# Holding the second block's weight loads and row gathers behind a run-time branch

## The chip, the cores and the metric

The kernel runs on one core of one Trainium2 chip. The metric is device time of one execution in microseconds (us). TensorE (PE in the profile) does the matmuls and transposes, VectorE (DVE), ScalarE (ACT) and GpSimd (POOL) the rest; SyncE (SP) issues the plain DMA transfers, GpSimd the gathers and scatters. Each engine takes its instructions in the order of the program. All transfers share 16 DMA engines.

## The reference, cut to what matters

Three layers follow each other: sparse attention over 1152 tokens of 512 features, a layer that sends each token to one of eight experts, and a dense layer in which four experts are mixed. The change touches the second alone:

```python
for e in range(8):                      # _moe_ref
    mask = argmax(logits, axis=1) == e
    h = np.maximum(x[mask] @ w1[e], 0.0)           # w1[e]: 512 x 1024
    out[mask] = gate_w[mask, None] * (h @ w2[e])   # w2[e]: 1024 x 512
```

How many tokens an expert gets is known only at run time.

## The kernel before, in words

Tokens are sorted on the chip into slots. The two fullest experts are **blocks** k = 0 and 1, of four row groups each (464 rows). Slot `S_ONE` is a **single tile** of 128 rows (k = 2). Two **small tiles** hold 32 rows each of further experts. What then remains goes to **overflow tiles**, which run only when the counted number of tiles (`ntl`) asks for them. `overflow()` (L1520 to L1532) loads `ntl` into every engine's registers (L1522) and opens nested `tc.If` (L1527); with these inputs no overflow tile is needed and every engine jumps over the body. The body is long, and it uses the second half of the staging memory, `raws[4:]`, as its own weight buffers, with TensorE and ScalarE among its readers and writers.

A weight block is 512 KB. SP loads it into one of eight staging places `raws[0..7]` (`load_block`, L197). `Weights.ahead` (one block per call here) then **splits** it: ScalarE rounds it to `wh` (L1169), VectorE subtracts to get `wl` (L1170), and the staging place is free for the next load. Blocks are numbered in the order of use: 0 to 7 belong to block k = 0 and use all eight places; 8 to 15 (k = 1) and 16 to 23 (k = 2) use `raws[0..3]` only, since the small tiles stream their weights through `raws[4..7]`, in the order of the ring. `W.ready` says how many blocks may be loaded at all; `Weights.load` issues as many as have a free place.

Work on TensorE is a list of turns, `l1(k, fb)` (12 matmuls, first layer, L1597 to L1599) and `l2(k, c)` (12 matmuls, second layer, L1616 to L1618). After each turn `tick(k, fb, n)` does what `todo` has at that point, then calls `W.ahead` once, then advances the small tiles by one piece (`next(small)`). So at tick (0, 5, 1) the branch is taken; at (0, 6, 0) the first row group of block 1 is transposed and split (`x_split` 0, L1174, L1169, L1170) and after it weight block 12 is split; (0, 6, 1) has `x_split` 1, (0, 7, 0) `x_split` 2 and the split of block 13, (0, 7, 1) `x_split` 3. All four use one PSUM bank `PA[0]`: TensorE can transpose group 2 only when VectorE has read group 1.

Row gathers are indirect DMAs by GpSimd. `gathered` (L1638) fetches rows, `with_rows` (L738) fetches the gate columns. `second_rows` gathers the four groups of block 1; `small_rows` those of the small tiles and of the single tile; `gates` the seven gate columns.

Of the kernel before, what the change touches and what calls it, by code (L numbers as in the profile page):

```python
# [28 lines left out]
KC = DM // P  # L29
FC = FF // P  # L30
# [20 lines left out]
NSM = 2  # L51
SM = 32
S_ONE = 2 * NBT
# [91 lines left out]
def fused_kernel(  # L145
# [53 lines left out]
    def expert_value(ap):  # L199
        return nc.values_load(  # L200
            ap,
            engines=[ET.SP],
            min_val=0,
            max_val=E1 - 1,
            skip_runtime_bounds_check_because="clipped on chip",
        )
# [529 lines left out]
    def with_rows(y, idx, n=NTOK):  # L736

        nc.gpsimd.indirect_dma_start(  # L738
            out=y[:, DM:], out_offset=None, in_=xx[:n, :], in_offset=bass.IndirectOffsetOnAxis(ap=idx, axis=0)
        )  # L740
# [435 lines left out]
    def x_split(x, i, g, pt):  # L1176
        w = P if i < NBT - 1 else LAST
        transposed(g, pt)
        src = pt.rearrange("p (c n) -> p c n", c=KC)[:, :, :w]
        split(*(t[:, :, P * i : P * i + w] for t in x), src)  # L1180
# [105 lines left out]
    W = Weights(m1b + m2b, raws, len(m1b), FC)  # L1286
# [10 lines left out]
    def x2_load(j):  # L1297
        g = gp.tile([P, XW], F32, name="g")
        eng = nc.gpsimd if j < CHT[0] else nc.sync
        eng.dma_start(out=g, in_=xc[P * j : P * (j + 1), :])  # L1300
        gx[j] = g
# [201 lines left out]
    for _ in fill:  # L1503
        pass
    W.owner[KC:] = [None] * (RAW - KC)
    W.ready = len(W.blocks)
    W.load()
    ectx.close()
    HT.append([x2p.tile([P, 2, max(CHT), 2, HP], F32R, name=n) for n in ("hh2a", "hl2a")])
# [4 lines left out]
    with ExitStack() as mctx:  # L1514
# [3 lines left out]
        mp = mctx.enter_context(tc.tile_pool(reuse_waits="tile", name="mp", bufs=1))  # L1518
        og, oy = (mp.tile([P, XW], F32, name=n) for n in ("og", "oy"))

        def overflow():
            ntl = nc.values_load(  # L1522
                ntl_i[0:1, 0:1], min_val=0, max_val=NSX, skip_runtime_bounds_check_because="bounded by the token count"
            )
            assert W.ns >= 2 * KC
            ow = raws[KC:]
            with ExitStack() as more:  # L1527
                more.enter_context(tc.If(ntl > S_OVF))
                for t in range(S_OVF, NSX):
                    if t > S_OVF:  # L1530
                        more.enter_context(tc.If(ntl > t))
                    over_tile(expert_value(main.etab[t : t + 1, 0:1]), at(t), main.dest[:, t : t + 1], ow)  # L1532
# [45 lines left out]
        X, G, H = {0: xA}, {0: gA}, {}  # L1578
# [52 lines left out]
        def at(slot):  # L1631
            return main.idx[:, slot - NBT : slot - NBT + 1]

        def gathered(slots, pool, name, bufs):
            res = []
            for t in slots:
                g = pool.tile([P, XW], F32, name=name, bufs=bufs)
                nc.gpsimd.indirect_dma_start(  # L1638
                    out=g[:, :DM], out_offset=None, in_=xe, in_offset=bass.IndirectOffsetOnAxis(ap=t, axis=0)
                )  # L1640
                res.append(g)
            return res

        def with_all(gs, slots):
            for g, t in zip(gs, slots):
                with_rows(g, t)
# [78 lines left out]
        def copies():  # L1725
            pr = PA[1][:, 64 : 64 + NSM]
            for q in range(P // SM):
                nc.tensor.matmul(pr[SM * q : SM * (q + 1)], ident[:, :SM], main.idxf, start=True, stop=True)
            nc.vector.tensor_copy(idxs, pr)

        def steps(n):
            for _ in range(n):
                next(rest)

        slotsB = []
        slots_s = [idxs[:, n : n + 1] for n in range(NSM)]
# [4 lines left out]
            slotsB.extend(at(NBT + i) for i in range(NBT))  # L1741
            G[1] = gathered(slotsB, gp, "g", None)

        def small_rows():
            copies()
            G["s"] = gathered(slots_s, mp, "sg", NSM)
            G[2] = gathered([at(S_ONE)], mp, "sone", 1)

        def gates():
            with_all(G[1], slotsB)  # L1750
            with_all(G["s"], slots_s)
            with_all(G[2], [at(S_ONE)])

        def branch():
            nonlocal small
            overflow()
            X[1] = [mp.tile([P, KC, NBW], F32R, name=n) for n in ("xbh", "xbl")]
            small = small_tiles()
            next(small)

        small = None
        todo = {
            (0, 0, 0): lambda: (steps(2), with_all(gA, [idx4[:, i : i + 1] for i in range(NBT)])),
            (0, 1, 0): lambda: steps(2),
            (0, 2, 0): lambda: steps(3),
            (0, 4, 0): second_rows,
            (0, 4, 1): small_rows,
            (0, 5, 0): gates,
            (0, 5, 1): branch,
            (1, 1, 0): lambda: [x2_load(j) for j in range(CHT[0])],  # L1770
        }
        for i in range(NBT):
            todo[0, 6 + i // 2, i % 2] = lambda i=i: x_split(X[1], i, G[1][i], PA[0])
        todo[1, 6, 1] = split_one
        for j in range(CHT[0]):
            prep[j] = x2_prep(j)
            todo[1, 3 + (j + 2) // 2, j % 2] = lambda j=j: [0 for _ in prep[j]]
# [1 line left out]
        def tick(k, fb, n):  # L1779
            early_ = (k, fb) < (0, 4)  # L1780
            if early_:
                W.ahead(RING, 1)
            todo.get((k, fb, n), lambda: None)()
            if not early_:
                W.ahead(RING, 1)
            if (k, fb, n) >= (0, 6, 1):
                next(small, None)

        steps(1)
# [7 lines left out]
        for n, (f, i) in enumerate(turn):  # L1797
            f(*divmod(i, FC))
            n += n > 0
            n += n > 2  # L1800
            tick(*divmod(n // 2, FC), n % 2)
# [270 lines left out]
```

## Time and profile before

| | |
|---|---|
| median of 3 runs | 597.32 us (593.5 to 598.12) |
| the profiled execution | 593.85 us, its span 592.1 us |
| granted TensorE clock, mean | 0.99 |
| TensorE busy | 571.2 us, 96% of the span |
| weight load into TensorE busy | 481.2 us, 81% |
| VectorE, ScalarE, GpSimd busy | 363.3, 284.2, 222.6 us |
| DMA moved | 77.56 MB, mean 131 GB/s |

Times in the profile count from the start of the span. Busy shares say little about one spot: the branch occupies a few microseconds near 105 us of 592, and what happens there is read from the instructions and waits of that stretch. A name such as ACTq or PEldq is the sequencer of an engine: its branches, register loads and semaphore instructions.

### The profile page before, as it was taken

The page shows a single profiled execution, that of the slowest core. Times are in us where ns is not written, and L with a number is a line of the kernel's source. Part 1 is how long each engine was busy: PE and PEld are TensorE (multiplying, and loading weights), DVE is VectorE, ACT ScalarE, POOL GpSimd, SP SyncE. Part 2 cuts the span into 40 slices and gives each one's busy share as a digit, 9 for nine tenths or more (in the row PEclk, how much of TensorE's full clock was granted, in tenths as well). Part 3 has the DMA queues.
Part 4 walks back from the last instruction along what each step waited for, and adds up shares of the span by engine and source line. Part 5 has one row for each costly group of instructions (what it writes and reads, how often), then busy time and mean ns, then how long its engine had stood idle before and what let it go on. Part 6 is the DMA issues. An engine that isn't in the chain of part 4 may idle for free.

```text
span 592.1 us, 10100 instructions
## 1 busy us (share of the span) xinstructions
PE 571.2 (96%) x3746; PEld 481.2 (81%) x3746; DVE 363.3 (61%) x767; ACT 284.2 (48%) x617; POOL 222.6 (38%) x316
## 2 busy tenths in 40 slices
PE   8997999799999999999999999999999999999994
PEld 4555778677788878988889889999988999998883
DVE  5775788433473856776776866755575575566531
ACT  5764263333454645565665654544444444444410
POOL 6624232704212552475666664322223222222212
PEclk9999999899999999999999999999999999999998
DMA  8956643798822535323314223222332122221001
GB/s 257 321 142 227 193 128 124 222 370 296 286 76 71 198 143 166 138 73 107 107 73 143 72 78 136 75 104 90 119 112 72 71 72 72 71 72 72 0 19 71
DMA packets 33664, 77.56 MB, mean 131 GB/s; under 512 B 5858, under 2 KB 11884, under 8 KB 33479
## 3 DMA queue, kind: packets, MB, share of 16 engines
q1 hardware_dynamic: 28583, 65.66, 33.1%
q0 software_dynamic: 4736, 10.99, 5.6%
q8 instruction: 31, 0.51, 0.3%
q14 instruction: 26, 0.21, 0.1%
q10 hardware_dynamic: 288, 0.19, 0.1%
HBM read 73.46 MB, written 7.55 MB: 137 GB/s over the span
## 4 chain that ended last, share of the span: by engine, by line
PE 63%; issue 1%; ACT 0%; POOLq 0%; DVE 0%; ACTq 0%; POOL 0%
PE ps_b L1439 10%; PE ps_b L1440 10%; PE ps_b L1441 10%; PE ps_b L1894 7%; PE ps_b L1893 7%; PE ps_b L1896 7%; PE ps_a L1894 4%; PE ps_a L1893 4%; PE ps_a L1896 4%; PE ps_a L1174 0%; POOLq L2067 0%; ACT wh L1360 0%; DVE xl L1459 0%; DVE stage L1906 0%; ACT xh L1457 0%
## 5 line engine op out<-in xcount | busy, mean ns | idle before, releaser
L1361 DVE TENSOR_TENSOR wl<-stage,wh 128x512 fp32r<-128x512 f32 (+1 forms) x160 | 124.3, 778 | 56.0 <-ACT wh L1360 55.4
L1360 ACT CAST wh<-stage 128x512 fp32r<-128x512 f32 (+1 forms) x160 | 102.9, 664 | 2.9 <-DMA stage<-in_w2b_dram 2.2
L1381 POOL TENSOR_TENSOR stage<-stage 128x256 f32<-128x256 f32 x32 | 24.1, 752 | 212.1 <-DVE wl L1361 212.1
L1439 PE MATMUL ps_b<-x,wh 128*128 128x320 f32 x224 | 69.8, 312 | 0.2 <-DVE xl L1459 0.2
L1440 PE MATMUL ps_b<-x,wh 128*128 128x320 f32 x224 | 69.2, 309 | 0.0
L1441 PE MATMUL ps_b<-x,wl 128*128 128x320 f32 x224 | 69.1, 308 | 0.0
L1451 DVE TENSOR_TENSOR m2t<-ps_b,stage 128x320 f32<-128x320 f32 (+1 forms) x93 | 42.2, 454 | 39.6 <-PE ps_b L1441 38.1
L1439 PE MATMUL ps_b<-xh,wh 128*128 128x256 f32 x224 | 64.0, 286 | 1.8 <-ACT stage L1472 1.2
L1441 PE MATMUL ps_b<-xh,wl 128*128 128x256 f32 x224 | 63.0, 281 | 0.0
L1440 PE MATMUL ps_b<-xl,wh 128*128 128x256 f32 x224 | 63.0, 281 | 0.0
L1439 PEld LDWEIGHTS ps_b<-xh,wh 128*128 128x128 f32 x224 | 42.3, 189 | 8.1 <-ACT stage L1472 1.6
L1439 PEld LDWEIGHTS ps_b<-x,wh 128*128 128x128 f32 x224 | 42.0, 188 | 5.4 <-DVE xl L1459 0.4
L1440 PEld LDWEIGHTS ps_b<-x,wh 128*128 128x128 f32 x224 | 42.1, 188 | 4.5
L1440 PEld LDWEIGHTS ps_b<-xl,wh 128*128 128x128 f32 x224 | 42.2, 188 | 4.1
L1441 PEld LDWEIGHTS ps_b<-xh,wl 128*128 128x128 f32 x224 | 42.3, 189 | 0.0
L1441 PEld LDWEIGHTS ps_b<-x,wl 128*128 128x128 f32 x224 | 42.1, 188 | 0.0
L1454 ACT ACTIVATE hh2b<-m2t 128x256 fp32r<-128x256 f32 (+1 forms) x45 | 19.9, 443 | 44.7 <-DVE m2t L1451 41.0
L1454 ACT ACTIVATE hh2a<-m2t 128x256 fp32r<-128x256 f32 (+1 forms) x42 | 18.7, 445 | 44.6 <-DVE m2t L1451 44.6
L1170 DVE TENSOR_TENSOR wl<-stage,wh 128x1024 fp32r<-128x1024 f32 x24 | 29.3, 1223 | 11.4 <-ACT wh L1169 11.2
L1894 PE MATMUL ps_b<-wl,hh2b 128*128 128x512 f32 x90 | 35.7, 397 | 0.0
L1893 PE MATMUL ps_b<-wh,hh2a 128*128 128x512 f32 x90 | 35.6, 395 | 0.0
L1894 PE MATMUL ps_b<-wl,hh2a 128*128 128x512 f32 x90 | 35.6, 395 | 0.0
(396 smaller groups left out, 1397.9 us busy)
## 6 DMA issues: line engine op xcount, KB each, us to landing
stage<-in_w1b_dram SPq DMA_DIRECT2D x32, 512.0 KB
stage<-in_w2b_dram SPq DMA_DIRECT2D x32, 512.0 KB
stage<-in_w1a_dram SPq DMA_DIRECT2D x24, 512.0 KB
stage<-in_w2a_dram SPq DMA_DIRECT2D x24, 512.0 KB
g<-xc SPq DMA_DIRECT2D x5, 260.0 KB
vl<-in_vlo_dram SPq DMA_DIRECT2D x2, 520.0 KB
g<-xc POOLq DMA_DIRECT2D x4, 260.0 KB, 6.0
xe<-rw POOLq DMA_DIRECT2D x7, 128.0 KB, 5.5
```

The lines of the kernel that those rows point to most:

```text
L1170: nc.vector.tensor_tensor(dst_l, src, dst_h.bitcast(F32), op=ALU.subtract)
L1360: return (lambda: nc.scalar.copy(h[:, s], src[:, s])), (lambda: nc.vector.tensor_tensor(l[:, s], src[:, s], h[:, s].bitcast(F32), op=ALU.s ...
L1361: lambda: nc.vector.tensor_tensor(l[:, s], src[:, s], h[:, s].bitcast(F32), op=ALU.subtract)
L1381: nc.gpsimd.tensor_tensor(a22, a22, a21, op=ALU.add)
L1439: nc.tensor.matmul(ph, wh[:, kc], xh, start=first and kc == 0, stop=False, skip_group_check=True)
L1440: nc.tensor.matmul(ph, wh[:, kc], xl, start=False, stop=False, skip_group_check=True)
L1441: nc.tensor.matmul(ph, wl[:, kc], xh, start=False, stop=kc == 1, skip_group_check=True)
L1451: nc.vector.tensor_tensor(t, a, b, op=ALU.add)
L1454: nc.scalar.activation(h, a, AF.Relu)
L1893: nc.tensor.matmul(po, hh, wh, start=(fb == 0 and fh == 1), stop=False, skip_group_check=part)
L1894: nc.tensor.matmul(po, hh, wl, start=False, stop=False, skip_group_check=part)
L1896: nc.tensor.matmul(po, hl, wh, start=False, stop=last, skip_group_check=part)
```

## The change

It moves work across the branch at tick (0, 5, 1), and changes no arithmetic. Ahead of the branch only 12 weight blocks (0 to 11) may be loaded, and only the four gathers of block 1's rows are issued. Behind it come, in the order of the program: the gathers of the small tiles, the first four weight loads of the first small tile, the further blocks from 12 on, the gate columns, the gather of the single tile. The pieces of the small tiles begin at tick (0, 7, 0) rather than (0, 6, 1), behind `x_split` 2, and the single tile's rows are split at (1, 7, 0) rather than (1, 6, 1).

```diff
-    W.ready = len(W.blocks)
+    W.ready = FC + KC
...
-        def small_rows():
-            copies()
-            G["s"] = gathered(slots_s, mp, "sg", NSM)
-            G[2] = gathered([at(S_ONE)], mp, "sone", 1)
-
-        def gates():
-            with_all(G[1], slotsB)
-            with_all(G["s"], slots_s)
-            with_all(G[2], [at(S_ONE)])
-
         def branch():
             nonlocal small
             overflow()
+            G["s"] = gathered(slots_s, mp, "sg", NSM)
             X[1] = [mp.tile([P, KC, NBW], F32R, name=n) for n in ("xbh", "xbl")]
             small = small_tiles()
             next(small)
+            W.ready = len(W.blocks)
+            W.load()
+            with_all(G["s"], slots_s)
+            with_all(G[1], slotsB)
+            one = [at(S_ONE)]
+            G[2] = gathered(one, mp, "sone", 1)
+            with_all(G[2], one)
...
-            (0, 4, 1): small_rows,
-            (0, 5, 0): gates,
+            (0, 4, 1): copies,
             (0, 5, 1): branch,
...
-        todo[1, 6, 1] = split_one
+        todo[1, 7, 0] = split_one
...
-            if (k, fb, n) >= (0, 6, 1):
+            if (k, fb, n) >= (0, 7, 0):
                 next(small, None)
```

## Rows read from the trace of the kernel before

**Rows 1.** The page, busy time of each engine.
```profile
PE 571.2 (96%) x3746; PEld 481.2 (81%) x3746; DVE 363.3 (61%) x767; ACT 284.2 (48%) x617; POOL 222.6 (38%) x316
```

**Rows 2.** Stretches: length; PE, PEld, DVE, ACT, POOL busy (counts); clock, DMA share, GB/s.
```profile
105.57:108.83 3.26, 0.00 (x1) 0.00 (x0) 0.01 (x1) 0.00 (x0) 2.65 (x3) 1.00 0.94 327
108.83:112.39 3.56, 3.56 (x10) 3.06 (x11) 1.23 (x1) 1.05 (x1) 2.65 (x4) 0.52 0.72 270
...
114.00:119.00 5.00, 5.00 (x28) 4.21 (x27) 2.96 (x4) 2.28 (x4) 2.67 (x3) 1.00 0.78 202
119.00:124.00 5.00, 5.00 (x36) 3.50 (x36) 2.46 (x3) 1.98 (x3) 0.00 (x0) 1.00 1.03 301
124.00:160.00 36.00, 36.00 (x287) 27.15 (x285) 13.34 (x21) 13.93 (x25) 9.61 (x18) 1.00 0.94 337
```

**Rows 3.** Waits of PE from 90 to 215 us: total, times, longest.
```profile
PE ps_b L1597 <- ACTq L1527: 3.3, 1, 3.3
```

**Rows 4.** Instructions of the branch line: count, ns min/median/max, first and last start.
```profile
L1527 PEldq COMPARE_BRANCH  x1: 6452/6452/6452, 102.0 to 102.0; - x1
L1527 ACTq COMPARE_BRANCH  x1: 50/50/50, 103.4 to 103.4; - x1
...
L1527 PEldq EVENT_SEMAPHORE  x1: 51/51/51, 108.5 to 108.5; - x1
L1527 ACTq EVENT_SEMAPHORE  x1: 17/17/17, 108.8 to 108.8; - x1
...
L1527 POOLq INC_SWDGE_SEM  x1: 1076/1076/1076, 122.9 to 122.9; - x1
```

**Rows 5.** DMA queues, 105 to 106 us: packets, MB, share; instruction packets are code.
```profile
q8 instruction: 1, 0.02, 5.8%
```

**Rows 6.** The same view, 106 to 107 us.
```profile
q14 instruction: 1, 0.01, 2.3%
```

**Rows 7.** ScalarE in time order: start, us, line, operation [idle before].
```profile
108.85 1.05 ACT L1169 CAST wh<-stage 128x1024 fp32r<-128x1024 f32 x1 [4.53 <-ACTq L1527]
...
113.67 0.58 ACT L1169 CAST xbh<-ps_a 128x512 fp32r<-128x512 f32 x1
114.14 1.07 ACT L1169 CAST wh<-stage 128x1024 fp32r<-128x1024 f32 x1
116.89 0.58 ACT L1169 CAST xbh<-ps_a 128x512 fp32r<-128x512 f32 x1 [1.68 <-PE ps_a L1174]
```

**Rows 8.** VectorE in time order, the same columns.
```profile
115.24 1.23 DVE L1170 TENSOR_TENSOR wl<-stage,wh 128x1024 fp32r<-128x1024 f32 x1 [0.19 <-ACT wh L1169]
117.50 0.69 DVE L1170 TENSOR_TENSOR xbl<-ps_a,xbh 128x512 fp32r<-128x512 f32 x1 [1.04 <-ACT xbh L1169]
```

**Rows 9.** TensorE in time order, the same columns.
```profile
105.17 0.40 PE L1618 MATMUL ps_b<-wh,hl 128*80 128x512 f32 x1
108.83 0.67 PE L1597 MATMUL ps_b<-xh,wh 128*128 128x464 f32 x1 [3.26 <-ACTq L1527]
...
116.69 0.60 PE L1174 MATMUL ps_a<-mk,sg 128*128 128x128 f32 x4
117.04 0.46 PE L1597 MATMUL ps_b<-xh,wh 128*128 128x464 f32 x1
...
119.66 0.60 PE L1174 MATMUL ps_a<-mk,g 128*128 128x128 f32 x4
```

**Rows 10.** SP's DMA issues in time order; the last row merges four.
```profile
94.47 0.33 SPq L197 DMA_DIRECT2D stage<-in_w1a_dram  x1
100.37 0.33 SPq L197 DMA_DIRECT2D stage<-in_w2a_dram  x1
...
105.60 0.33 SPq L197 DMA_DIRECT2D stage<-in_w2a_dram  x1
114.02 2.70 SPq L197 DMA_DIRECT2D stage<-in_w1a_dram  x4
```

**Rows 11.** The row gathers of line 1638, issue to landing, all seven.
```profile
DMA to landing us min/median/max: 3.3/7.4/7.7
```

## The prediction

> **What bounds the kernel now.** I read the busy times first: TensorE is busy 571.2 us of the 592.1 us span [rows 1], so nearly everything is matmul time, and a change that moves no matmul can win only where TensorE stands still or is slowed. The waits of TensorE come next: in the middle of the program one of 3.3 us stands out, at the first matmul after the branch, put down to ScalarE's branch [rows 3]. TensorE's last matmul ahead of it starts at 105.17 and its next one at 108.83 [rows 9]. The table by stretch shows the rest of the price: no matmul from 105.57 to 108.83, and then 3.56 us at a granted clock of 0.52, that is for most of it the lower level, 1.2 GHz [rows 2]. That costs 3.56 x 0.48 = 1.7 us more. The branch is worth 3.3 + 1.7 = 5.0 us, 0.8% of the time; nothing else here offers more, since from 114 to 160 us TensorE is busy throughout, with the DMA engines at 0.78 to 1.03 of their time [rows 2].
>
> Why it costs that: TensorE's branch instruction alone took 6.45 us, from 102.0 to 108.5. ScalarE's branch was over in 0.05 us at 103.4, but its next instruction came at 108.8 [rows 4]. Code travels on the same DMA engines as data: a 16 KB packet of code moved between 105 and 106 us and another one between 106 and 107 us, three to four microseconds after the two branches [rows 5, 6], in a stretch where the DMA share was 0.94 [rows 2]. That traffic is weight blocks 12 to 14, which SP issued from 100.37 to 105.60 [rows 10], and the row gathers.
>
> **The change, part by part.** *Ahead of the branch* go away: three loads (blocks 12, 13, 14), three row gathers and seven gate gathers. SP then has nothing between block 11 (94.47) [rows 10] and its own branch; it gets there some 10 us sooner and waits at the first load of the small tile, because that load fills a staging place which the overflow body uses too, so it can go only when TensorE and ScalarE are past the branch. The four gathers of block 1's rows stay in flight. TensorE reaches its branch at the same time as before, for no instruction of its own ahead of it is moved.
>
> Call R the time at which TensorE resumes. Upper bound: 108.8, as before. Lower bound: 105.6, where TensorE runs dry anyhow [rows 9]. Between them I go by the gathers, which shared those DMA engines: 3.3 us at best, 7.4 us in the middle [rows 11]; the code took 5.4 us from ScalarE's branch. With 3.3 us for a fetch, ScalarE is back at 103.4 + 3.3 = 106.7 and TensorE's own fetch at 102.0 + 3.3 = 105.3, so **R = 106.7**, a wait of 1.1 us. That is 2.1 us gained, and the 1.7 us of slow clock would go too if so short a wait lets the clock stand.
>
> The Trainium skill speaks against even this part: its page "DMA: Bandwidth & Descriptors", section "Queues, rings and completion order", says that each DMA engine takes turns between the queues packet by packet, so code would not stand behind a whole weight block. By that rule the fetch is long by itself and R stays near 108.8; the late code packets [rows 5, 6] speak for the queue instead, without settling it.
>
> *Behind the branch* the loads come in this order: four blocks of the small tile, then 12, 13, 14. Before, block 12 was loaded at 100.37, long ahead of use. Now it is fifth in line. What is queued behind it is the point. ScalarE and VectorE take instructions in order: after group 0 of block 1 (113.67) ScalarE splits block 12 (114.14), and only then comes group 1 (116.89) [rows 7]; VectorE subtracts in the same order, 115.24 and 117.50 [rows 8]. TensorE may not transpose group 2 (119.66) [rows 9] until VectorE has read group 1. So block 12's landing holds x_split 2, whatever TensorE could do.
>
> When does it land? Before, the loads behind the branch began at 114.02 [rows 10]. Five blocks are 2.62 MB; at 202 and 301 GB/s for 5 us each, 2.52 MB were through at 124, and the rest at 337 GB/s by 124.3 [rows 2]: 10.3 us after the first issue, and 11 with something for the completion. Lower bound 8.8: all at 337 GB/s (7.8) plus 1. Upper bound 13.4: the three gathers that now follow the branch on GpSimd (0.79 MB) go in between at the same rate, 2.3 us more. I take 11, since before some gate gathers were in the way as well.
>
> After the landing: cast 1.07, subtraction 1.23, subtraction of group 1 0.69 [rows 7, 8], and 0.1 for signals: 3.1 us. So x_split 2 starts at R + 11 + 3.1 = 106.7 + 14.1 = **120.8**. TensorE alone would be there at R + 8.8 = 115.5: before it took 119.66 - 108.83 = 10.8, less 1.7 for the slow clock and 0.35 for the small tile's transposes (116.69 to 117.04) [rows 9], which now follow x_split 2. A wait of 5.3 us thus takes the place of the one shortened. The comparable time before is 119.66 - 0.35 = 119.3, so TensorE is **1.5 us late** from here on. Such a wait can bring the slow clock back as the first did, 0 to 1.7 us; I take 0.9. With the bounds: from 105.6 + 8.8 + 3.1 = 117.5 (1.8 us early) to 108.8 + 13.4 + 3.1 = 125.3 (6.0 late, 7.7 with the clock).
>
> *The rest costs nothing, for reasons that can fail.* The gathers of the small tiles go out when GpSimd is past its own branch. It waits there for the gathers in flight and then signals for 1.08 us; that signal came at 122.9 before because fourteen gathers were out [rows 4]. Now it is four, the last at about 103, so some 107 + 1.1, and the small tile's first rows land at about 109 + 3.3 to 7.7 [rows 11], that is 112 to 117, ahead of 120.8. Without the wait for block 12 they could cost up to 1.5 us. The gate columns are wanted when results are scaled, tens of microseconds later. The small tile's half step gives its weights, which follow at 337 GB/s, about a turn more of time. The single tile's rows are split one turn ahead of its first matmuls, not two: a turn is about 2.6 us (117.04 to 119.66) [rows 9] against a cast and a subtraction of 0.6 to 0.7 each [rows 7, 8]. Nothing after x_split 2 is shorter than before, so the delay is carried to the end by a TensorE that is busy.
>
> **The sum.** 2.1 + 1.7 us won at the branch, about 5.3 + 0.9 us paid at x_split 2: net **+2.4 us**. The profiled execution took 593.85 us (span 592.1 and 1.75 around it), below the median of 597.32; the four executions shown lie between 593.5 and 598.12, with a mean of 595.7. From the profiled one the sum gives 596.3, from the median 599.7; I predict from the mean: **598.1 us**.
>
> **Rivals.**
> *The gain is kept.* Block 12 lands in time, because the loads behind the branch run ahead of my row, or are not in line. Then x_split 2 starts at 115.5 (R = 106.7) or 114.4 (105.6): 3.8 to 4.9 us won, 590.8 to 591.9 us. For it: the DMA engines have room, a share of 0.72 from 108.83 to 112.39 with loads and gathers that now are elsewhere [rows 2]. Against: four blocks stand in front of 12 in one queue, and 8.8 us is the best their bytes allow.
> *The fetch is not relieved* (slower). If code is late by its own latency and not by the queue, R = 108.8, the loads start as late, and x_split 2 starts at 108.8 + 14.1 = 122.9: 3.6 late, 5.3 with the slow clock, 601.0. It is over 1% (6 us) slower once block 12 needs 11.7 us or more rather than 11; with 13.4 it is 7.7 late, 603.4. For it: both code packets moved some three to four us after their branches, though they left at different times [rows 4 to 6]. Against: gathers more than doubled their time in the same stretch [rows 11]. This is what the rule of the Trainium skill named above would give.
> *The loads are not held.* If the small tile's first load does not wait for TensorE and ScalarE, SP sends four blocks from about 98 us on, the DMA engines are as full at the branch as before, R = 108.8, and block 12 is there in time: no change, 595.7. Against: the staging places shared with the body.
>
> **How the numbers follow.** About 1% is what a measurement of this kernel can tell from no change. Forecast (second wait, some net loss or none): 0.58. Gain kept: 0.20, all within 1%. Fetch not relieved: 0.14, half of it beyond 1%. Loads not held: 0.08. Of the forecast's own range, 1.8 early to 7.7 late, about a tenth lies beyond 6 us. So slower 0.13, faster 0.04 (the gain at its largest, measured against a high run), same 0.83. The range goes from 592.5 (most of the gain) to 603 (nearly all of the late end).
>
> **What would show it.** TensorE's wait at the first L1597 behind the branch falls from 3.3 to about 1 us, and the clock after it stays at its higher level. ScalarE shows an idle time of some 5 us ahead of a 128x1024 cast of L1169, released by the load of a w2 block, and TensorE a wait at a transpose of L1174. No such wait on ScalarE proves my second half wrong; an unchanged 6.45 us at TensorE's branch proves the first half wrong. It would also fail if GpSimd, which now comes to its branch some 9 us sooner, stood there for code as the others do.

## The result, and the profile after

The changed kernel takes **599.26 us** (median of 10 runs, 597.77 to 602.25) beside 593.72 us for the kernel before in the runs taken with it: ratio **1.0098, 95% interval 1.0074 to 1.0121**. It is about 1% slower, and the interval leaves no room for no change. Ratios here leave out executions in a slower state, and medians count all, which matters for one kernel below, where two of twelve executions took 794 and 927 us. The profiled execution took 597.77 us with a span of 596.0 us, 3.9 us more than before.

First the waits of TensorE from 90 to 220 us (in total, times, longest):

```profile
PE ps_a L1174 <- DVE xbl L1170: 6.8, 1, 6.8
PE ps_b L1439 <- ACT stage L1472: 1.3, 1, 1.3
PE ps_b L1597 <- ACTq L1527: 1.0, 1, 1.0
PE ps_b L1439 <- DVE hl2a L1459: 0.6, 1, 0.6
```

The wait at the branch fell from 3.3 us [rows 3] to 1.0. A new one of 6.8 us stands at a transpose of L1174. The two at L1439 were there before, with 1.2 and 0.6 us. The branch itself (durations in ns, then the starts):

```profile
L1527 PEldq COMPARE_BRANCH  x1: 3592/3592/3592, 101.0 to 101.0; - x1
L1527 ACTq COMPARE_BRANCH  x1: 50/50/50, 102.4 to 102.4; - x1
...
L1527 ACTq EVENT_SEMAPHORE  x1: 17/17/17, 105.5 to 105.5; - x1
L1527 POOLq INC_SWDGE_SEM  x1: 876/876/876, 105.7 to 105.7; - x1
```

TensorE's branch took 3.6 us where it took 6.45, ScalarE was back after 3.1 us and not 5.4, and GpSimd gave its signal at 105.7 and not 122.9 [rows 4]. This execution comes to the branch 1.0 us earlier than the one before (101.0 against 102.0); that is the spread from one execution to another, for block 11's load, ahead of everything that was moved, is already 0.94 us earlier (93.53, shown below, against 94.47 [rows 10]). So **the stretch from the branch to the end costs 3.9 + 1.0 = 4.9 us**. Where they go is seen in ScalarE's and VectorE's order (start, us, line, operation, idle before):

```profile
105.63 1.05 ACT L1169 CAST wh<-stage 128x1024 fp32r<-128x1024 f32 x1 [2.28 <-ACTq L1527]
...
108.90 0.58 ACT L1169 CAST xbh<-ps_a 128x512 fp32r<-128x512 f32 x1
118.50 1.04 ACT L1169 CAST wh<-stage 128x1024 fp32r<-128x1024 f32 x1 [9.03 <-DMA stage<-in_w2a_dram]
119.45 0.58 ACT L1169 CAST xbh<-ps_a 128x512 fp32r<-128x512 f32 x1
```

```profile
119.58 1.23 DVE L1170 TENSOR_TENSOR wl<-stage,wh 128x1024 fp32r<-128x1024 f32 x1 [9.31 <-ACT wh L1169]
120.72 0.68 DVE L1170 TENSOR_TENSOR xbl<-ps_a,xbh 128x512 fp32r<-128x512 f32 x1
```

ScalarE has nothing to do for 9.0 us until block 12 has landed at 118.5, and only then casts row group 1, which TensorE had transposed long since. Before, these two casts came at 114.14 and 116.89 [rows 7]. TensorE's own order, and the loads on SP:

```profile
105.61 0.47 PE L1597 MATMUL ps_b<-xh,wh 128*128 128x464 f32 x1 [1.01 <-ACTq L1527]
...
121.46 1.12 PE L1174 MATMUL ps_a<-mk,g 128*128 128x128 f32 x4 [6.84 <-DVE xbl L1170]
```

```profile
93.53 14.75 SPq L197 DMA_DIRECT2D stage<-in_w1a_dram  x5
108.57 0.34 SPq L197 DMA_DIRECT2D stage<-in_w2a_dram  x1
109.48 0.35 SPq L197 DMA_DIRECT2D stage<-in_w1a_dram  x1
110.05 1.47 SPq L197 DMA_DIRECT2D stage<-in_w2a_dram  x2
```

The first row merges block 11 and the four small blocks; SP was past its branch at 98.4 us and then stood at the first small load until the branch was behind TensorE and ScalarE. Block 12 goes out fifth, at 108.57, and three more loads follow within 3 us of it. By stretch (length; PE, PEld, DVE, ACT, POOL busy; clock, DMA share, GB/s):

```profile
90.00:127.00 37.00, 29.15 (x151) 23.19 (x150) 19.05 (x30) 12.48 (x17) 14.67 (x15) 0.91 0.61 198
105.57:108.83 3.26, 3.22 (x17) 2.90 (x18) 1.22 (x1) 1.44 (x2) 1.39 (x1) 1.00 0.62 183
108.83:112.39 3.56, 3.56 (x20) 2.80 (x19) 1.24 (x2) 0.65 (x2) 2.72 (x3) 1.00 0.95 291
112.39:120.00 7.61, 2.23 (x11) 1.65 (x9) 0.42 (x1) 1.50 (x3) 5.78 (x7) 0.83 1.04 361
...
121.46:124.30 2.84, 2.84 (x11) 2.65 (x12) 1.31 (x3) 1.69 (x3) 0.00 (x0) 0.50 0.69 223
```

The second and third of these lines are the stretches that were empty, and then slow at a clock of 0.52, before [rows 2]: now TensorE works through both at full clock. The idle time has moved into the stretch after them, and the slow clock behind it: 0.50 (1.2 GHz) from 121.46 to 124.30. So 2.3 us of wait and 1.7 of clock were won at the branch, and 6.8 of wait and 2.84 x 0.50 = 1.4 of clock lost at `x_split` 2: net 4.2 of the 4.9 us. Read by position it is nearly all: `x_split` 2 starts at 121.46 + 1.0 = 122.4 in the time of the execution before, where it stood at 119.66 with the small tile's transposes (0.35) [rows 9] already done, so 3.1 late; with 1.4 of clock, and 0.3 at L1832 and L1439 later on, 4.8.

### The profile page after: what moved, and what is told of

It is laid out like the page before. It is cut to its first block, busy times and chain, and to the rows that moved or that the text cites. A ratio compares the mean times of both kernels' runs of the same rounds, so it can differ in the third digit from the quotient of the medians.

```text
span 596.0 us, 10094 instructions
## 1 busy us (share of the span) xinstructions
PE 568.8 (95%) x3746; PEld 479.5 (80%) x3746; DVE 363.2 (61%) x767; ACT 284.6 (48%) x617; POOL 221.3 (37%) x316
## 4 chain that ended last, share of the span: by engine, by line
PE 62%; issue 1%; ACT 0%; POOLq 0%; DVE 0%; POOL 0%; ACTq 0%
PE ps_b L1439 10%; PE ps_b L1440 9%; PE ps_b L1441 9%; PE ps_b L1891 7%; PE ps_b L1890 7%; PE ps_b L1893 7%; PE ps_a L1891 4%; PE ps_a L1890 4%; PE ps_a L1893 4%; PE ps_a L1174 0%; POOLq L2064 0%; ACT wh L1360 0%; DVE xl L1459 0%; ACT xh L1457 0%; ACT hh2b L1454 0%
## 5 line engine op out<-in xcount | busy, mean ns | idle before, releaser
L1439 PE MATMUL ps_b<-x,wh 128*128 128x320 f32 x224 | 69.7, 311 | 0.2 <-DVE xl L1459 0.2
L1439 PE MATMUL ps_b<-xh,wh 128*128 128x256 f32 x224 | 63.9, 285 | 1.9 <-ACT stage L1472 1.3
L1439 PEld LDWEIGHTS ps_b<-xh,wh 128*128 128x128 f32 x224 | 42.2, 189 | 8.3 <-ACT stage L1472 1.7
L1439 PEld LDWEIGHTS ps_b<-x,wh 128*128 128x128 f32 x224 | 42.0, 187 | 5.4 <-DVE xl L1459 0.4
```

The costliest lines, as they stand in the source:

```text
L1439: nc.tensor.matmul(ph, wh[:, kc], xh, start=first and kc == 0, stop=False, skip_group_check=True)
```

## The experiments

They ran on three chips (4, 1 and 7), where the kernel before took 597.45, 597.71 and 598.47 us, some 4 us more than the 593.72 beside the result. Times that I expected were set on the lower level, so they are to be read with that shift; each ratio is against runs of it on the same chip. Each profile is one execution, so places and waits are read from it, and whether a kernel is faster from the ratio.

**The weight loads ahead again, the gathers held** (`weights_ahead`).

```diff
-    W.ready = FC + KC
+    W.ready = len(W.blocks)
...
-            W.ready = len(W.blocks)
-            W.load()
```

> The changed kernel with its hold on the weight loads undone: blocks 12 to 14 are loaded ahead of the branch again, the gathers stay behind it. My theory (the loss is block 12 standing fifth in line behind the branch): the 6.8 us wait of TensorE at x_split 2 is gone, and the time is at or below the kernel before (593.7 us), 591 to 594 us. How much of the branch wait comes back tells what delays the code: if it is the weight loads, TensorE waits 2.5 us or more there again; if it is the gathers, about 1 us as in the changed kernel (591 to 592 us). Rival (the later pieces of the small tiles or the later gathers cost the time, not block 12): 597 us or more.

Measured: 597.83 us, ratio 1.0022 (0.999 to 1.0053). TensorE's waits from 90 to 127 us, then the branch of TensorE and of ScalarE:

```profile
PE ps_b L1597 <- ACTq L1527: 3.2, 1, 3.2
PE ps_a L1174 <- issue: 3.1, 1, 3.1
```

```profile
L1527 PEldq COMPARE_BRANCH  x1: 5992/5992/5992, 99.8 to 99.8; - x1
L1527 ACTq COMPARE_BRANCH  x1: 50/50/50, 101.2 to 101.2; - x1
...
L1527 ACTq EVENT_SEMAPHORE  x1: 17/17/17, 106.5 to 106.5; - x1
```

The loads alone bring the long branch back: TensorE's takes 5.99 us, and ScalarE is back after 5.3 us instead of 3.1. ScalarE no longer waits for block 12, and the time is that of the kernel before, as far as the interval can tell; the rival's 597 us is reached only because the kernel before itself takes 597.45 here. What I had not expected is the second wait: `x_split` 2 still stands 3.1 us, now because ScalarE's cast of group 1 stood 5.94 us, and not for a load. More on it below.

**The gathers ahead again, the weight loads held** (`gathers_ahead`). The mirror image: `small_rows` and `gates` (the rows of the small tiles and of the single tile, and all gate columns) back at their ticks, `W.ready` as in the change.

> The changed kernel with only the weight loads held: the gathers of the small tiles and the single tile and all gate columns go ahead of the branch as in the kernel before. My theory (place in the line): block 12 still has four blocks in front of it and TensorE still waits 4 us or more at x_split 2; landing 10 to 11.5 us after the first load instead of 12.9, since three gathers less are in the way; 596 to 599 us. Rival (the gathers behind the branch made block 12 late): the wait at x_split 2 is 2.5 us or less and the time 594 us or less. At the branch: if the gathers delay the code, TensorE waits 2.5 us or more; if the weight loads do, about 1 us.

Measured: 601.68 us, ratio 1.0086 (1.0052 to 1.012).

```profile
PE ps_a L1174 <- DVE xbl L1170: 7.6, 1, 7.6
PE ps_b L1597 <- PEq L1527: 1.3, 1, 1.3
```

```profile
L1527 PEldq COMPARE_BRANCH  x1: 4752/4752/4752, 100.0 to 100.0; - x1
L1527 ACTq COMPARE_BRANCH  x1: 50/50/50, 101.4 to 101.4; - x1
L1527 ACTq EVENT_SEMAPHORE  x1: 17/17/17, 104.5 to 104.5; - x1
```

```profile
118.49 1.04 ACT L1169 CAST wh<-stage 128x1024 fp32r<-128x1024 f32 x1 [9.75 <-DMA stage<-in_w2a_dram]
```

TensorE's branch took 4.75 us, the wait behind it only 1.3, and ScalarE was back after 3.1 us as in the changed kernel. So of the two things that were moved behind the branch, the weight loads carry the shorter branch and the loss; the gathers show little of either. One expectation failed: block 12 landed 13.5 us after the first small load (105.02) and not 10 to 11.5. The gathers were issued earlier, but 0.81 MB of them still moved between 104.8 and 118.5.

**Blocks 12 and 13 second in line** (`second_in_line`). Only the order of the loads behind the branch is changed: one small block, then 12 and 13, then the other small ones.

```diff
-            for _ in ring:
-                load()
+            for n in range(len(ring)):
+                load()
+                W.ready = FC + KC + min(n + 2, 3)
+                W.load()
```

> The changed kernel with the loads behind the branch in another order: one block of the small tile, then blocks 12 and 13, then the second of the small tile, 14, and the small tile's last two. All of them still wait for the branch. My theory: block 12 lands some 6 us after the first load instead of 12.9, TensorE's wait at x_split 2 falls from 6.8 us to 1.5 us or less, the wait at the branch stays near 1.0 us, and the time is 588.5 to 591 us, below both kernels. Rival (the transfers behind the branch are too many for the time left, whatever their order): a wait of 3 us or more turns up at another instruction, for the small tile's weights or a later block, and the time stays at 594 us or more.

Measured: 595.65 us, ratio **0.9968 (0.9937 to 0.9999)**; run once more on a third chip 594.73 us, **0.9939 (0.9897 to 0.9981)**:

> second_in_line once more, on the same chip as the kernel with the gates late. Theory A: the wait of 4 to 5 us at the fourth x_split (or the third) stands again; ratio 0.995 to 0.998. Theory C: the wait is gone or elsewhere, and the ratio is within 0.002 of that of the kernel with the gates late.

The second execution: ScalarE in time order, the wait of TensorE from 90 to 127 us, and the table of that stretch:

```profile
112.04 1.05 ACT L1169 CAST wh<-stage 128x1024 fp32r<-128x1024 f32 x1 [2.04 <-DMA stage<-in_w2a_dram]
113.00 0.58 ACT L1169 CAST xbh<-ps_a 128x512 fp32r<-128x512 f32 x1
```

```profile
PE ps_b L1597 <- ACTq L1527: 0.8, 1, 0.8
```

```profile
90.00:127.00 37.00, 36.21 (x211) 27.64 (x210) 21.70 (x32) 14.38 (x20) 15.76 (x15) 1.00 0.65 212
```

This is the test of the cause. The branch keeps its gain, ScalarE waits 2.0 us for block 12 instead of 9.0, no transpose waits, the clock is 1.00 throughout, and TensorE is busy 36.2 of 37 us where the change had 29.2 at a clock of 0.91. Block 12 lands 5.9 us after the first small load, and 6.1 in the first execution, as expected. With one thing moved the loss is gone: on the first chip every run (590.96 to 598.8) is below every run of the `gathers_ahead` (600.21 to 603.99), which has the change's order of loads. That it is faster than the kernel before is shown too, by 0.3 and 0.6%, but not that the shorter branch is the reason: two kernels below beat the kernel before with the old order of loads. The time that I expected, 588.5 to 591, is 2.7 to 5.2 us below the 593.7 of the kernel before; measured against it on the same chip, the first 12 runs are only 1.8 us below and the repeat 3.7. Something is paid: the small tile's later blocks now come behind 12 and 13, and in this trace TensorE waits for them after 127 us.

```profile
PE ps_a L1703 <- DMA stage<-in_w2a_dram: 1.9, 2, 1.3
```

The first execution had no wait at `x_split` 2 either, but one of 4.8 us at `x_split` 3, behind a cast that stood 4.36 us for "remote" (see the last section). That is more than the 3 us which I had set for the rival, though not for a load, as the rival had it. In the second execution no transpose waits, so theory A of the repeat did not come; theory C's 0.002 was missed narrowly (0.9939 against 0.9914 below, the intervals overlapping).

**The kernel before without its branch** (`no_branch`). `overflow()` left out, so the overflow tiles could never run.

> The kernel before without the overflow branch: the tiles that would run only for other inputs are left out, and nothing else is. Prices the branch. My theory: TensorE's 3.3 us wait and the slow clock after it (1.7 us) vanish, 5.0 us less than the kernel before, 588 to 589.5 us. Rival (the wait is hidden by other work or turns into another one): 591 us or more.

Measured: 596.35 us, ratio 0.9987 (0.9965 to 1.0009). The 5 us that I had priced the branch at did not come, and the rival did: the wait at L1597 is gone, and TensorE stands 4.0 us at `x_split` 2 instead.

```profile
PE ps_a L1174 <- issue: 4.0, 1, 4.0
```

```profile
116.05 0.59 ACT L1169 CAST xbh<-ps_a 128x512 fp32r<-128x512 f32 x1 [7.17 <-remote]
```

**The half step alone, in the kernel before** (`half_step`).

```diff
-        todo[1, 6, 1] = split_one
+        todo[1, 7, 0] = split_one
...
-            if (k, fb, n) >= (0, 6, 1):
+            if (k, fb, n) >= (0, 7, 0):
```

> The kernel before with the half step alone: small tiles from the third and not the second half step behind the branch's, the single tile half a step later; loads and gathers as before. By the theory that the half step is hidden: ratio 0.998 to 1.002, the wait at the branch 3.4 us as before and no new one over 1 us. By the rival that the half step itself makes the later work wait (the small tiles' loads come free half a step later, the single tile is split nearer to its use): ratio 1.004 to 1.008, with a wait of 2 us or more past 130 us that the kernel before does not have.

Measured: 596.18 us, ratio 0.9973 (0.9949 to 0.9997): no loss in it, rather a small gain that I had not expected and that the trace doesn't explain. Two expectations for its trace failed: the wait at the branch is 2.1 us and not 3.4, and a new one of 3.3 us stands at `x_split` 2, behind a late signal (last section). Its trace also has a wait of 1.5 us at L1439 (for `hl2a`) that is 0.5 to 0.6 in the traces without the half step, and 0.6 to 1.5 in those with it; that is under the 2 us that I had set for the rival, and the times don't show it.

**The changed kernel and the kernel before, once more, for their traces** (`after_again`, `before_again`).

> The changed kernel as it is, beside the others. By the theory that block 12's late landing is the whole of the loss (branch won 2.3 us and 1.7 us of slow clock, x_split 2 waits 6.8 us and 1.7 us of slow clock): the wait at x_split 2 is 6.3 to 7.6 us behind the cast of block 12, which lands 12.5 to 13.5 us after the first small load; ratio to the kernel before 1.006 to 1.011. If the late signals of TensorE of weights_ahead and no_branch are in every kernel here, ScalarE's copies wait for TensorE and not for the load, and the ratio is under 1.004.

> The kernel before as it is, for its trace beside the others. If late signals of TensorE come with a chip or a recording, ScalarE's copy at x_split 1 to 3 waits 4 to 7 us for TensorE here too (111 to 122 us), and TensorE waits for it; if they come with the order of transfers in no_branch, weights_ahead and second_in_line, the branch's wait of 3.4 us stands as in the first trace and no wait over 1.5 us follows it before 125 us. Time 594 to 599.

Measured: the changed kernel 599.56 us, ratio 1.0035 (1.0013 to 1.0057); it waits 6.6 us at `x_split` 2, with ScalarE held 8.8 us by the load. The kernel before, one run, 597.84 us:

```profile
PE ps_b L1597 <- ACTq L1527: 2.9, 1, 2.9
PE ps_a L1174 <- DVE xbl L1170: 2.1, 1, 2.1
PE ps_a L1680 <- DMA stage<-in_w1a_dram: 0.7, 2, 0.4
```

```profile
119.91 0.59 ACT L1169 CAST xbh<-ps_a 128x512 fp32r<-128x512 f32 x1 [4.30 <-PE ps_b L1599]
```

The load's wait is nearly the same in both traces of the changed kernel (8.8 and 9.0 us), and so are the two times (599.56 and 599.26); the ratio is below the 1.006 to 1.011 that I had expected because the kernel before is slower here (597.71 us against 593.72). Its trace has a wait at `x_split` 2 that its first trace did not have; whether that accounts for the 4 us, one execution can't show. ScalarE's cast is put down to matmuls of L1599, but the transposes it reads had started at 115.65. So a late signal stands in a kernel whose order of transfers was never touched.

**The gates late** (`gates_late`, `gates_again`; `gates_only`). To `second_in_line`, twice, and then to the kernel before, one thing is added: the gate gathers stand at tick (1, 0, 0) in the program.

> As second_in_line (the changed kernel with blocks 12 and 13 of the second block fetched right behind the first small load), and the gates of the small tiles, of the second block and of the single tile, with the gather of the single tile's row, are issued at the first half step of the second block (about 130 us) and not at the branch. Theory A, the gates' many small packets (about 111 to 118 us) and the loads behind the branch together hold up TensorE's signals: the wait of 4.8 us at the fourth x_split, which stood in second_in_line, is gone, and its slow clock of some 1.7 us with it; time 589 to 591, 1.0 to 1.4% below the kernel before. Theory B, the loads alone hold the signals up, wherever the gates are: a wait of 4 to 5 us for ScalarE's copy behind a signal of TensorE stays at x_split 3 or 2; time 595 to 597. Theory C, the wait belongs to those runs on that chip and to nothing in the order of the transfers: it may stand or not, and then in the kernel before as well.

> The kernel with blocks 12 and 13 second in line and the gates late once more, beside second_in_line on the same chip. Theory A: no wait over 1.5 us at the x_splits, ratio 0.990 to 0.995, some 2 to 4 us under second_in_line. Theory C: no difference to second_in_line that the interval can tell, and its x_split waits may show in the trace.

> The kernel before with one thing moved: the ten or so gate gathers (second block, small tiles, single tile) are issued at the first half step of the second block, about 130 us, and not at the sixth step of the first; loads, branch, row gathers and half step as before. Theory A, GpSimd's gate gathers after the branch hold up signals on the chips of these studies (in the kernel before's trace there, ScalarE's copy at x_split 2 waited 4.3 us and TensorE 2.1 us for it, while GpSimd issued gates from 109 to 119 us): no wait over 1 us at the x_splits, the branch's wait of 2.9 to 3.4 us stays; ratio to the kernel before 0.994 to 0.997. Theory C, the late signals have nothing to do with the gates: a wait of 2 to 5 us at an x_split is seen as before, ratio 0.998 to 1.002.

Measured: with `second_in_line` 593.82 us, ratio 0.9938 (0.9909 to 0.9966), and 592.79 us, **0.9914 (0.988 to 0.9948)**, the fastest here; with the kernel before 594.58 us, 0.9948 (0.9914 to 0.9983). But in `second_in_line` the edit hardly did what it says. GpSimd's first gate gather of block 1 in `second_in_line`, and with the gates late:

```profile
112.34 0.94 POOL L738 DMA_INDIRECT g<-xx,idx  x1 [0.30 <-issue]
```

```profile
111.55 0.95 POOL L738 DMA_INDIRECT g<-xx,idx  x1 [0.30 <-issue]
```

GpSimd had nothing to wait for between the two places in the program, so the gates went out no later than before. In the kernel before they moved by some 5 us (107.95 to 113.21), for there GpSimd's own branch now stands ahead of them. That kernel, GpSimd and the one wait of TensorE from 90 to 127 us:

```profile
113.21 0.94 POOL L738 DMA_INDIRECT g<-xx,idx  x1 [7.28 <-DMA g<-xe,idx]
```

```profile
PE ps_b L1597 <- ACTq L1527: 3.1, 1, 3.1
```

This is what theory A had: no wait at an `x_split`, the branch's wait as before, a ratio within 0.994 to 0.997. But one trace can't carry it, because kernels that issue their gates at the same times differ as much: TensorE's wait at an `x_split` behind a late signal is 4.8 us and nothing in the two traces of `second_in_line`, and nothing and 1.5 us in the two with the gates written later (besides 1.0 and 0.8 us there behind block 12). The third chip has `second_in_line` with and without the late gates, 592.79 and 594.73 us, with overlapping intervals. So theory A is not shown.

The kernels with blocks 12 and 13 early in line beat the kernel before in all four comparisons, but so do two that keep the old order and the loads ahead of the branch: the half step alone (0.9973) and the gates late (0.9948). The latter is as fast as `second_in_line` on the same chip, 594.58 and 594.73 us, with its 3.1 us at the branch. So what the order of the loads costs is shown, and what the shorter branch is worth by itself is not. For some worth of it speaks that on the first chip `second_in_line`, at 595.65 us, is below the kernel with the weight loads ahead, at 597.83; but their intervals overlap a little.

## Why the prediction was right or wrong

The forecast was 598.1 us, with a loss too small to tell as the likeliest; the time is 599.26, inside the range. The loss is at the edge of the 1% that I took for what a measurement can tell, but the interval is about four times finer, so it is a loss. The mechanism came out as written, and its second term too small.

- *The branch.* R was put at 106.7 with a wait of 1.1 us. Measured: 105.61, or 106.6 in the time of the execution before, and a wait of 1.0. The fetch took 3.1 and 3.6 us where the fastest gather gave 3.3 [rows 11]. That a gather's landing time prices a fetch of code is argued and not shown; the number held. (The second code packet, [rows 6], is 0.01 MB and not 16 KB; no term hangs on it.) The clock stood, as assumed.
- *SP held at the first small load.* Right: past its branch at 98.4, five loads only from 105.6 on. The rival in which they are not held falls.
- *The landing of block 12, the mis-sized step.* It was put at 11 us after R, with a bound of 13.4. It took 118.50 - 105.61 = **12.9**. My sum counted the five blocks in line, 2.62 MB. The stretches after the branch carry more: 183 GB/s for 3.26 us, 291 for 3.56 and 361 for 6.1 are 3.8 MB by 118.5. Counted by queue, 3.22 MB of it are weight loads, six blocks' worth, and 0.54 MB gathers: loads issued behind block 12 and the gathers moved beside it. A place in line says when a load starts, not that nothing behind it takes a share.
- *From the landing to `x_split` 2* I had 3.1 us; measured 121.46 - 118.50 = 3.0. The wait is 6.8 and not 5.3 us, `x_split` 2 is 3.1 us late and not 1.5, and the clock behind it cost 1.4 and not 0.9. Together 4.5 us and not 2.4; with the 0.3 at L1832 and L1439 that makes 4.8 of the 4.9.
- *The rest at nothing.* The small tile's rows landed by 115.1, ahead of use, and GpSimd came to its signal with no stand of its own. The half step cost nothing that a time shows.
- *The level.* I put the sum on a mean of 595.7 us for the kernel before; beside the result its median is 593.72, on the three chips of the experiments 597.5 to 598.5. Between the medians the loss is 5.5 us. So the sum was 3.1 us short and the base 2.0 us high, and that 598.1 came so near to 599.26 is in good part luck.
- *The fetch is not relieved* had the fetch independent of the weight loads, R at 108.8. The traces speak against it: ScalarE came back 3.0 to 3.1 us after its branch in all seven traces with the weight loads held, and 4.3 to 5.4 us in all five with weight loads ahead of it. TensorE's branch took 5.99 us with the loads ahead of it and the gathers held, 4.75 with only the gathers ahead, and 3.6 with neither; with loads and row gathers ahead it was 6.45, 5.77, 5.63 and once 4.85, so it is a tendency with a spread, not a fixed price for each block. The rival leaned on the Trainium skill ("DMA: Bandwidth & Descriptors", section "Queues, rings and completion order"). What it states, that each DMA engine takes turns between its queues packet by packet, no run here tests. What falls is the conclusion that the fetch would then not feel the loads.
- *The gain is kept*, my first rival, was held to be 0.20 likely. It did not come, but `second_in_line` shows that another order of the same loads brings the short wait at the branch without the loss.

## What to carry to other kernels

When loads are held back behind a point, list them in the order in which they will be needed after it, and put the first one that an in-order engine will meet at the head; what was fetched long ahead of use has no margin any more. A wait that is removed is worth its length only as far as the next thing that engine needs is there: here some 4 us were won at the branch and 8 lost behind it, by where one block stood in a queue. An instruction that is to start later must have something to wait for; a later line in the program isn't enough on an engine that runs ahead.

## What the runs showed that I had not expected

**Signals that come late.** In six of the eleven traces of the experiments, the kernel before's among them, ScalarE stands idle 3.8 to 7.2 us ahead of a cast of an `x_split`, with no load to wait for. The plainest is `half_step`, TensorE and then ScalarE, and all engines in between (columns as in the table by stretch above):

```profile
112.52 0.60 PE L1174 MATMUL ps_a<-mk,g 128*128 128x128 f32 x4
...
117.56 0.58 ACT L1169 CAST xbh<-ps_a 128x512 fp32r<-128x512 f32 x1 [6.10 <-remote]
```

```profile
113.20:117.50 4.30, 2.46 (x12) 1.85 (x10) 0.00 (x0) 0.00 (x0) 2.23 (x3) 1.00 0.15 16
```

The four transposes are over at 113.1, ScalarE and VectorE do nothing at all for 4.3 us, and the cast starts at 117.56 ("remote": released by a signal whose source the trace doesn't have). The DMA share is 0.15, so a full set of DMA engines isn't the reason here; in the same place of `no_branch` it is 1.1 (114 to 116 us). GpSimd issues gate gathers in this stretch, as it does in the first trace of the kernel before without such a wait. The traces of the two kernels that stand at the start, [rows 7] and the first section's, don't have it. What delays the signal, and whether it would be there in an execution that isn't recorded, is open. Because of it one profile alone could not decide between `second_in_line` and the change, and it may be why the branch left out gave nothing: in that trace ScalarE's 7.17 us and TensorE's 4.0 us come from it.

**A taken branch has no fixed price.** TensorE's took 3.6 to 4.1 us in five traces with neither weight loads nor the further gathers ahead of it and 4.7 in a sixth, 4.75 with the gathers alone, and 4.85 to 6.45 in five traces with weight loads ahead. By itself that hardly separates the cases; ScalarE's return, 3.0 to 3.1 against 4.3 to 5.4 us, does.
